# A chunk of V transposes moved ahead of the sum of exponents on TensorE

## The chip, the cores and the metric

The kernel runs on one core of one Trainium2 chip. The metric is device time in microseconds, the median of several executions of the same program. "Granted clock" is the share of TensorE's full speed that the throttle lets through.

## The reference

Attention for one query row and its backward pass: 32 heads, 8192 keys, head size 128, bf16.

```python
def _fwd_reference(q, k, v):
    scale = q.shape[-1] ** -0.5
    scores = jnp.einsum('bhqd,bhkd->bhqk', q, k) * scale
    attn = _softmax(scores, axis=-1)
    return jnp.einsum('bhqk,bhkd->bhqd', attn, v)
# outputs: out_0 = attention, out_1 = dq, out_2 = dk, out_3 = dv (for a given grad_out)
```

For each head K and V are read once (2 MB each), and dK and dV are written once (2 MB each). dK is an outer product of ds and q, dV an outer product of p and grad_out, so nearly all the bytes are these four tiles. PSUM is where the program has TensorE put its results; here ScalarE copies the transposed V out of it.

## The kernel before

One head is one turn of a loop, and the end of head h-1 (ds, dK, dq) is woven into the front of head h. The instruction order on each engine is the order of the program text. The parts that matter here:

```python
K_BUFS = 3
V_BUFS = 2
# ... PSUM pool for the transposed V: two buffers, psT ... bufs=2
def v_transposes(h, c):                        # c is one of four chunks of V
    T_ps = psT.tile([P, CH // 2, P], F32, tag="T", name="T_ps")
    # ... eight transposes on TensorE into T_ps
    X = tpool.tile([P, CH // 2, P], F32, tag="XT", name="XT_sb")
    nc.scalar.copy(X[:], T_ps[:])              # ScalarE empties the buffer
    XV[h, c] = X
# ... in the loop, for head h:
    nc.tensor.transpose(x["m"][:, 128:256], top[:].to_broadcast([P, P]), ident_f[:])  # row maxima
    # ... nbias (VectorE), then the exponent on ScalarE, with its row sums rs
    nc.scalar.activation(e[:], x["sn"], ACT.Exp, bias=nbias[:], scale=scale, accum_out=rs[:])
    nc.tensor.matmul(x["m"][:, 0:1], lhsT=ones_f[:], rhs=rs[:], ...)                  # sum of exponents
    # ... reciprocal rinv (VectorE), p = e * rinv (ScalarE), p_s (VectorE)
    v_transposes(h, 0)
    v_transposes(h, 1)
    v_transposes(h, 2)
    contract(Vt[h], x["p"], x["m"][:, 2:3])    # o = p V, 64 matmuls
    # ... v_scores (dp), v_transposes(h, 3), o . do, then dV products (VectorE) and the next V load
```

## Time and profile before

| what | before |
|---|---|
| time | 646.56 us, median of 3 (646.2 to 646.75) |
| TensorE, VectorE, ScalarE busy | 75%, 78%, 28% of the span |
| granted clock | 0.60 |
| bytes moved | 134.2 MB read, 134.2 MB written |
| transfers, most of the run | 422 to 433 GB/s |

No compute engine is busy all the time, the transfers are. Three rows of the view of the waits of the kernel before (who waited for whom: us in all, times, longest):

```profile
DVE G_dv L210 <- DMA out_dram<-G_dv: 84.6, 25, 4.6
...
PE s_ps L157 <- DVE pdt L234: 72.1, 24, 3.9
...
PE m_ps L294 <- ACT e L293: 40.5, 32, 1.3
```

The last row is the wait that the change aims at. The first two are larger and not touched by it.

### The profile page before, as it was taken

How to read it: one execution, taken by the hardware profiler on the slowest of the kernel's cores; microseconds unless marked ns; L12 is line 12 of the kernel's file. 1: busy time of each engine (PE TensorE's matmuls, PEld its weight loads, DVE VectorE, ACT ScalarE, POOL GpSimd, SP SyncE). 2: the span in 40 equal slices, each digit the busy share in tenths (PEclk: the TensorE clock that was granted, in tenths of full speed). 3: DMA queues.
4: the chain of work that ended last, by engine and by line, in shares of the span. 5: the costliest groups of instructions: out<-in, count | busy, mean ns of one | idle time of the engine just before them, and what ended most of it. 6: DMA issues, size and time to landing. Idle time of an engine off the chain costs nothing.

```text
span 644.5 us, 20935 instructions
## 1 busy us (share of the span) xinstructions
PE 481.0 (75%) x9673; PEld 452.0 (70%) x9673; DVE 505.5 (78%) x653; ACT 183.5 (28%) x332; POOL 0.7 (0%) x6
## 2 busy tenths in 40 slices
PE   3898888886677877768777787667786777877780
PEld 2888888886677866768666777667785676866670
DVE  5989899867977779777788777797767977778860
ACT  2333333332233222233222332223322223222230
POOL 0000000000000000000000000000000000000000
PEclk9766666655666655666556666556655666655665
DMA  8999999999999999999999999999999999999985
GB/s 349 407 425 430 424 425 423 429 426 431 427 428 427 427 427 429 429 429 425 433 422 433 425 430 427 427 429 425 427 429 425 431 425 429 429 427 430 424 365 238
DMA packets 19718, 269.80 MB, mean 419 GB/s; under 512 B 2352, under 2 KB 2352, under 8 KB 2864
## 3 DMA queue, kind: packets, MB, share of 16 engines
q1 hardware_dynamic: 19584, 268.47, 98.2%
q8 instruction: 75, 1.23, 0.7%
q14 instruction: 11, 0.09, 0.0%
q10 hardware_dynamic: 48, 0.01, 0.0%
HBM read 134.23 MB, written 134.23 MB: 417 GB/s over the span
## 4 chain that ended last, share of the span: by engine, by line
DMA 59%; PE 21%; DVE 14%; ACT 2%; issue 1%; SPq 0%; DVEq 0%; ACTq 0%
DMA Kt<-in_k_dram 48%; DVE XK_sb L146 8%; PE T_ps L183 8%; DMA out_dram<-G_dv 5%; DMA out_dram<-G_dk 5%; PE s_ps L157 5%; DVE G_dk L210 4%; PE dp_ps L200 3%; PE m_ps L200 2%; PE dp_ps L195 2%; ACT XT_sb L185 1%; PE m_ps L294 1%; DVE G_dv L210 1%; PE s_ps L173 1%; DVE sm L163 1%
## 5 line engine op out<-in xcount | busy, mean ns | idle before, releaser
L210 DVE TENSOR_TENSOR G_dv<-p_rep,qd 128x2048 bf16<-128x2048 bf16 x128 | 148.2, 1221 | 90.3 <-DMA out_dram<-G_dv 84.6
L183 PE MATMUL T_ps<-ident_f,Vt 128*128 128x128 f32 x1024 | 203.4, 382 | 0.2 <-PE m_ps L294 0.2
L183 PEld LDWEIGHTS T_ps<-ident_f,Vt 128*128 128x128 f32 x1024 | 190.7, 210 | 0.2 <-issue 0.2
L185 ACT COPY XT_sb<-T_ps 128x1024 f32<-128x1024 f32 x128 | 128.6, 1013 | 129.3 <-PE T_ps L183 127.2
L210 DVE TENSOR_TENSOR G_dk<-ds_rep,qd 128x2048 bf16<-128x2048 bf16 x128 | 155.6, 1218 | 2.9 <-DMA out_dram<-G_dk 1.9
L146 DVE STREAM_TRANSPOSE XK_sb<-Kt 128x1024 f32<-128x1024 f32 x128 | 148.3, 1214 | 5.8 <-DMA Kt<-in_k_dram 4.7
L157 PEld LDWEIGHTS <-XK_sb 128*128 128x128 bf16 x2048 | 57.7, 104 | 90.7 <-DVE pdt L234 79.9
L157 PE MATMUL s_ps<-q_blk,XK_sb 128*128 128x4 bf16 x2048 | 59.7, 168 | 82.1 <-DVE pdt L234 72.1
L195 PE MATMUL dp_ps<-do_blk,XT_sb 128*128 128x2 bf16 x2048 | 66.7, 164 | 18.1 <-ACT XT_sb L185 18.1
L195 PEld LDWEIGHTS <-XT_sb 128*128 128x128 bf16 x2048 | 64.9, 102 | 20.7 <-ACT XT_sb L185 20.7
L200 PE MATMUL dp_ps<-ds_rep,Kt 128*128 128x1 bf16 x2048 | 64.1, 165 | 1.3 <-issue 1.0
L200 PEld LDWEIGHTS <-Kt 128*128 128x128 bf16 x2048 | 59.6, 104 | 6.8 <-issue 6.6
L244 ACT COPY dq_all<-dp_ps 128x1 f32<-128x1 f32 x32 | 5.1, 159 | 192.4 <-PE dp_ps L200 178.5
L200 PEld LDWEIGHTS <-Vt 128*128 128x128 bf16 x2048 | 57.7, 97 | 0.9
L200 PE MATMUL m_ps<-p_rep,Vt 128*128 128x1 bf16 x2048 | 56.9, 164 | 0.0
L294 PEld LDWEIGHTS m_ps<-rs,ones_f 128*128 128x128 f32 x64 | 16.0, 311 | 49.9 <-ACT e L293 49.9
L294 PE MATMUL m_ps<-rs,ones_f 128*128 128x1 f32 x64 | 18.8, 362 | 40.5 <-ACT e L293 40.5
L303 ACT ACTIVATE p_rep<-e,rinv 128x256 bf16<-128x256 f32 x32 | 16.3, 508 | 30.1 <-DVE rinv L301 30.1
L163 DVE TENSOR_TENSOR sm<-s_ps,in_quad 128x256 f32<-128x256 f32 x32 | 13.6, 424 | 11.1 <-PE s_ps L157 7.9
L229 ACT CAST qd<-s_ps 128x256 bf16<-128x256 f32 x32 | 11.9, 372 | 32.2 <-PE s_ps L225 32.2
L236 DVE SCALAR_TENSOR_TENSOR ds_rep<-dp_ps,pdt,p_s 128x256 bf16<-128x256 f32 x32 | 15.5, 484 | 5.2 <-PE dp_ps L195 2.4
L293 ACT ACTIVATE e<-s_ps,nbias 128x64 f32<-128x64 f32 x32 | 10.0, 313 | 31.8 <-DVE nbias L290 31.8
(44 smaller groups left out, 143.4 us busy)
## 6 DMA issues: line engine op xcount, KB each, us to landing
Vt<-in_v_dram SPq DMA_DIRECT2D x32, 2048.0 KB, 30.0
Kt<-in_k_dram SPq DMA_DIRECT2D x31, 2048.0 KB, 30.8
out_dram<-G_dv SPq DMA_DIRECT2D x30, 2048.0 KB, 34.6
out_dram<-G_dk SPq DMA_DIRECT2D x30, 2048.0 KB, 33.6
out_dram<-G_dv SPq DMA_DIRECT2D x4, 1024.0 KB, 15.0
out_dram<-G_dk SPq DMA_DIRECT2D x4, 1024.0 KB, 13.3
Kt<-in_k_dram SPq DMA_DIRECT2D x4, 512.0 KB, 5.1
out_dram<-fin_sb SPq DMA_DIRECT2D x2, 8.0 KB, 13.1
```

What stands on the lines that cost most here:

```text
L146: nc.vector.transpose(XK[h][:, :, :, u, :], slots(Kt[h], u, NCH).rearrange("p g d -> p (g d)").bitcast(F32).rearrange("p (g w j) -> p g w ...
L157: nc.tensor.matmul(out[:, g, :], lhsT=cols[:, g, c // 2, c % 2], rhs=q_blk[:, h, c, :], start=(c == 0), stop=(c == 2 * NB - 1), skip_group ...
L163: nc.vector.tensor_tensor(x["sm"][:], x["s"][:, 0:NT].rearrange("p (a g) -> p a g", a=NQ).unsqueeze(2) .to_broadcast([P, NQ, NCH, CH]), in ...
L183: nc.tensor.transpose(T_ps[:, i, :], words[:, m * P:(m + 1) * P], ident_f[:])
L185: nc.scalar.copy(X[:], T_ps[:])
L195: nc.tensor.matmul(st[h]["dp"][:, n:n + 2], lhsT=X[:, i, e2, :], rhs=do_blk[:, h, e2, :], start=(e2 == 0), stop=(e2 == 1), skip_group_chec ...
L200: nc.tensor.matmul(out_col, lhsT=Xt[:, n, :], rhs=rep[:, n, 0:1], start=(n == 0), stop=(n == NT - 1), skip_group_check=True)
L210: nc.vector.tensor_tensor(slots(G, r, 4).rearrange("p n (a b) -> p n a b", b=R), slots(rep, r, 4).unsqueeze(2).to_broadcast([P, Q, D // R, ...
L229: nc.scalar.copy(x["qd"][:].rearrange("p a d -> p (a d)"), x["s"][:, 256:512])
L236: nc.vector.scalar_tensor_tensor(out=x["ds"][:], in0=x["dp"][:, 0:NT].unsqueeze(2).to_broadcast([P, NT, R]), scalar=pdt[:], in1=x["p_s"][: ...
L294: nc.tensor.matmul(x["m"][:, 0:1], lhsT=ones_f[:], rhs=rs[:], start=True, stop=True, skip_group_check=True)
L303: nc.scalar.activation(x["p"][:], e[:].unsqueeze(2).to_broadcast([P, NT, R]), ACT.Copy, scale=rinv[:])
```

## The change

TensorE stands still while ScalarE makes the exponent. The intent is to put eight V transposes into that gap, which need nothing of the softmax. Their copy out of PSUM must not stand in front of the p copy on ScalarE, so the copy is split off and stays where it was.

```diff
+    def v_copy(h, c):
+        X = tpool.tile([P, CH // 2, P], F32, tag="XT", name="XT_sb")
+        nc.scalar.copy(X[:], st[h].pop("T")[:])
+        XV[h, c] = X
-    def v_transposes(h, c):
+    def v_transposes(h, c, copy=True):
 ...
-        X = tpool.tile([P, CH // 2, P], F32, tag="XT", name="XT_sb")
-        nc.scalar.copy(X[:], T_ps[:])
-        XV[h, c] = X
+        st[h]["T"] = T_ps
+        if copy:
+            v_copy(h, c)
 ...
             nc.vector.tensor_reduce(nbias[:], x["m"][:, 128:256], axis=AX.X, op=ALU.max, negate=True)
+            v_transposes(h, 0, copy=False)
 ...
-        v_transposes(h, 0)
+        v_copy(h, 0)
         v_transposes(h, 1)
```

## The prediction

> **What bounds the kernel now.** I read the page from its chain and its slices first, then the DMA issues, then the cost groups of the lines that the change touches, then the timeline of one head and the busy time by stretches. The chain that ended last, the slices and the transfers:
>
> ```profile
> DMA  8999999999999999999999999999999999999985
> GB/s 349 407 425 430 424 425 423 429 426 431 427 428 427 427 427 429 429 429 425 433 422 433 425 430 427 427 429 425 427 429 425 431 425 429 429 427 430 424 365 238
> ...
> DMA 59%; PE 21%; DVE 14%; ACT 2%; issue 1%; SPq 0%; DVEq 0%; ACTq 0%
> ...
> Vt<-in_v_dram SPq DMA_DIRECT2D x32, 2048.0 KB, 30.0
> Kt<-in_k_dram SPq DMA_DIRECT2D x31, 2048.0 KB, 30.8
> out_dram<-G_dv SPq DMA_DIRECT2D x30, 2048.0 KB, 34.6
> ```
>
> The transfers run at 422 to 433 GB/s in slices 3 to 38 of 40, and a 2 MB load lands 30 us after it was issued. One head moves four such tiles (K, V, dK, dV): 4 x 2.097 MB / 428 GB/s = 19.6 us, and in the timeline the K transposes of consecutive heads begin 19.4 to 20.1 us apart (563.53, 582.97, 602.76). A tile alone needs 2.097 / 428 = 4.9 us, so 30 us are about six tiles in the queue: a backlog of 25 us that absorbs shifts of a microsecond in when a transfer is issued. The first six heads go at 17.25 us a head (K transposes at 21.04, 38.28, 55.53), held by compute, but they only eat the loads that were issued ahead; the slices show the transfers at full rate all the same.
>
> The groups that the change moves (line, engine, operation, count, busy us, mean ns, idle before):
>
> ```profile
> L183 PE MATMUL T_ps<-ident_f,Vt 128*128 128x128 f32 x1024 | 203.4, 382 | 0.2 <-PE m_ps L294 0.2
> L185 ACT COPY XT_sb<-T_ps 128x1024 f32<-128x1024 f32 x128 | 128.6, 1013 | 129.3 <-PE T_ps L183 127.2
> L294 PE MATMUL m_ps<-rs,ones_f 128*128 128x1 f32 x64 | 18.8, 362 | 40.5 <-ACT e L293 40.5
> ```
>
> TensorE waits 40.5 us over 32 heads, 1.27 us a head, for the exponent before the sum (L294). That is the gap that the change wants to fill. Head 30 in the timeline, a steady head:
>
> ```profile
> 563.52 0.34 SPq L78 DMA_DIRECT2D Vt<-in_v_dram  x1
> 591.56 0.48 PE L283 MATMUL m_ps<-ident_f,top 128*128 128x128 f32 x1
> 593.33 0.58 PE L294 MATMUL m_ps<-rs,ones_f 128*128 128x1 f32 x2 [1.29 <-ACT e L293]
> 593.77 5.36 PE L183 MATMUL T_ps<-ident_f,Vt 128*128 128x128 f32 x24
> 594.21 0.51 ACT L303 ACTIVATE p_rep<-e,rinv 128x256 bf16<-128x256 f32 x1 [0.94 <-DVE rinv L301]
> 597.95 4.63 DVE L210 TENSOR_TENSOR G_dv<-p_rep,qd 128x2048 bf16<-128x2048 bf16 x4 [3.47 <-DMA out_dram<-G_dv]
> 598.93 1.83 PE L200 MATMUL m_ps<-p_rep,Vt 128*128 128x1 bf16 x64
> ```
>
> The issue of this head's V stands in the first line. The view of that one transfer gives its time from issue to landing:
>
> ```profile
> DMA to landing us min/median/max: 29.3/29.3/29.3
> ```
>
> So V of head 30 landed at 563.52 + 29.3 = 592.8 us, but the transpose of the row maxima (L283) ended at 591.56 + 0.48 = 592.04. The moved chunk stands directly behind that transpose and needs V: **V is late by 0.8 us**. The same subtraction for every head gives V 0.6 to 1.4 us late in heads 7 to 31; only heads 0 to 6 have V early, by 0.3 to 10 us. The wait was invisible before, because the transposes stood behind the sum and started at 593.77.
>
> **What the Trainium skill says.** "DMA: Bandwidth & Descriptors", Specifications, gives a fabric ceiling of 435 GB/s for the 16 engines of a core; the trace's 428 GB/s is 98% of it, so there is no faster rate to be had by other timing. The same page, "Why a DMA increments its semaphore by 16 and not by 1", says that a transfer is done only when every engine that carries a part of it is done; the trace has no engine numbers, but the uneven end below fits. "TensorE: Matmul & The Clock Gate", Part 1, has a clock that is either half or full; the stretches show 0.50 and 1.00, and the chunk of eight transposes takes 1.07 us at 1.00 (at 621.95 us) and 1.7 us at 0.50 (614.31 us to the copy at 616.29, less 0.3 us of hand-over).
>
> **The change part by part.** The instruction order of the built kernel confirms: on TensorE eight transposes (chunk 0) move from behind the sum to between the maxima's transpose and the sum; ScalarE keeps its order (exponent, p copy, chunk 0 copy), since the copy of chunk 0 stood behind the p copy before too; VectorE's order is unchanged. Nothing is added or removed.
> - Steady head (times from the end of the maxima's transpose, before: sum at +1.29, first transposes +1.73, contraction at +6.9). After: chunk 0 waits for V to +0.8, runs 1.7 us to +2.5; the exponent was ready long before, so the sum is at +2.5, **1.2 us later**; chunk 1 from +2.95 to +4.65. Sum out at +3.1, reciprocal +3.4, p copy to +3.9, copy of chunk 0 (1.01 us) to +4.95. Chunk 2 needs the PSUM buffer that chunk 0 frees (two buffers), so it waits from +4.65 to +5.0 and ends at +6.6. Contraction at about +6.6: **0.3 us earlier**. p is 1.2 us later, but dV's VectorE work waits 3.47 us for the store of two heads ago anyway.
> - Early head (1 to 6): V is there, chunk 0 starts at once, sum 0.4 us later (1.7 - 1.29), contraction 0.3 to 0.4 us earlier. Here VectorE begins dV straight after p, so the dV products, the K transposes and ds come 0.4 us later, against only 0.2 us of VectorE idle before ds. The period may grow from 17.25 to about 17.5 us; five such heads, 1.5 us in all, go into the backlog, not into the time.
> - Last head: chunk 0 waits for V (1.1 us late), contraction 0 to 0.3 us earlier, and dK's products start at most that much earlier.
>
> The end, in stretches of the span (columns: PE, PEld, DVE, ACT, POOL busy, granted clock, DMA share, GB/s):
>
> ```profile
> 612.00:614.00 2.00, 0.64 (x3) 0.33 (x2) 2.00 (x4) 0.56 (x3) 0.00 (x0) 0.50 0.69 295
> 614.00:620.00 6.00, 6.00 (x45) 5.94 (x46) 2.25 (x5) 2.83 (x4) 0.00 (x0) 0.50 0.95 401
> 620.00:622.00 2.00, 2.00 (x84) 2.00 (x82) 2.00 (x2) 0.88 (x2) 0.00 (x0) 0.98 0.64 266
> ...
> 626.00:628.00 2.00, 1.48 (x46) 1.21 (x43) 2.00 (x3) 0.38 (x2) 0.00 (x0) 0.50 0.70 293
> 628.00:634.00 6.00, 0.00 (x0) 0.00 (x0) 1.96 (x2) 0.25 (x1) 0.00 (x0) 0.50 0.94 392
> 634.00:640.00 6.00, 0.00 (x0) 0.00 (x0) 0.00 (x0) 0.00 (x0) 0.00 (x0) 0.50 0.56 235
> ```
>
> Three times the queues run short (0.64 to 0.70), but never below about half, and from 634 to 640 us again about half of the engines work, 7 us after the other half is through. The likely reading: about nine engines are behind and never run dry, and they set the end. A dK issue that comes 0.3 us earlier then only feeds engines that finish early anyway. Sum: 0 us from the steady part, 0 to -0.3 us from the tail; 646.56 - 0.1 = 646.5 us.
>
> **The rivals.**
> 1. The gap is really gained: 1.27 us a head. For it: the 40.5 us of idle time. If it all counted, 606 us; but with transfers at 98% of their ceiling it can count only in the last head, whose chain from the landing of K (602.7) to the last product (630) is bare: at most 646.56 - 1.3 = 645.3 us. Against even that: V late, and the two PSUM buffers.
> 2. The wait for V starts a new chain: sum and p late by 1.2 us in 25 heads, then VectorE late, loads issued late. If nothing absorbed it, 646.6 + 25 x 1.2 = 677 us. Against it: 3.47 us of VectorE idle after p, a contraction that is not later, and 25 us of backlog.
> 3. The early heads slow down enough to starve the queue: 1.5 us at worst, 648 us. Against it: 430 GB/s in these slices.
>
> **Range and chances.** The runs before spread over 0.55 us (646.2 to 646.75). Rival 1 sets the low end, 645.3; rival 3 sets the high end, 647.8. Faster by 2% would need 633.6 us, which at 428 GB/s for 268.4 MB (627 us) leaves 6.5 us for start and tail, against some 19 now; slower by 2% needs 13 us that 25 us of backlog would have to let through. I give each 0.01.
>
> **What would show it.** In the changed trace: a new wait of TensorE for the V load before the first transposes, 0.6 to 1 us in some 25 heads, some 20 us in all; the idle time for the exponent before the sum near zero; a wait of 0.2 to 0.5 us a head before chunk 2 for ScalarE's copy; p later by about 1.2 us; VectorE's wait for the dV store shorter by about as much (84.6 us now, some 55 to 60 then); GB/s unchanged. Wrong would be: a contraction later than +7, slices below 420 GB/s in the steady part, or a tail in which all engines end together, earlier by over 0.5 us.

## The result, and the profile after

| what | before | after |
|---|---|---|
| time, median | 646.38 us of 4 (646.2 to 646.75) | 646.04 us of 4 (645.68 to 646.6) |
| ratio | | 0.9995, 95% interval 0.9977 to 1.0012 |
| span of the profiled run | 644.5 us | 644.6 us |

A ratio is the mean time of one kernel's runs over the mean of the other's runs of the same rounds, so it is not quite the ratio of the medians in the table. Executions over 1.5% slower than the fastest of the same kernel are left out of the means.

The page of the changed kernel (bytes per second by slice, chain, V transfers). Lines 188, 300 and 309 of the changed kernel are the transposes, the sum and the p copy, which were 183, 294 and 303:

```profile
GB/s 350 404 428 429 424 427 424 428 429 421 418 429 428 428 425 430 430 426 431 425 428 428 430 426 428 428 428 427 427 429 431 424 432 424 430 426 429 427 362 244
...
DMA 62%; PE 24%; DVE 9%; ACT 1%; issue 1%; SPq 0%; DVEq 0%; ACTq 0%
...
Vt<-in_v_dram SPq DMA_DIRECT2D x32, 2048.0 KB, 30.1
```

The rate by slice is about the same, and V still takes 30 us from issue to landing. Now the steady head 30 in the timeline of the changed kernel:

```profile
563.68 0.34 SPq L78 DMA_DIRECT2D Vt<-in_v_dram  x1
...
592.07 0.48 PE L288 MATMUL m_ps<-ident_f,top 128*128 128x128 f32 x1
...
593.32 1.94 PE L188 MATMUL T_ps<-ident_f,Vt 128*128 128x128 f32 x8 [0.77 <-DMA Vt<-in_v_dram]
...
595.05 0.42 PE L300 MATMUL m_ps<-rs,ones_f 128*128 128x1 f32 x2
...
598.17 4.63 DVE L215 TENSOR_TENSOR G_dv<-p_rep,qd 128x2048 bf16<-128x2048 bf16 x4 [2.13 <-DMA out_dram<-G_dv]
...
598.44 1.75 PE L205 MATMUL m_ps<-p_rep,Vt 128*128 128x1 bf16 x64
```

The eight transposes stand where they should, behind the transpose of the maxima, but wait 0.77 us for V. The sum comes 2.5 us after the maxima's transpose ends (592.55), where it was 1.29 us. VectorE's dV products then wait 2.13 us for the store of an earlier head where they waited 3.47. They begin when that store is done, whatever p does.

The view of the waits of the changed kernel, the rows that answer to the three above:

```profile
DVE G_dv L215 <- DMA out_dram<-G_dv: 52.8, 24, 3.6
...
PE s_ps L157 <- DVE pdt L239: 87.6, 31, 4.6
...
PE T_ps L188 <- DMA Vt<-in_v_dram: 24.7, 26, 2.5
```

The wait of the sum for the exponent is gone from the list. TensorE's two large waits were 72.1 + 40.5 = 112.6 us before and are 87.6 + 24.7 = 112.3 us now. **The idle time was not removed, it changed its name:** part of it is now a wait for V, and the rest a longer wait for VectorE before the K scores.

In the first six heads, where V is there early, the change does act. The timeline of the kernel before around the K scores of head 2 shows VectorE waiting twice in each head for TensorE (0.20 us at ds, in the prediction, and the row below):

```profile
45.85 0.42 DVE L163 TENSOR_TENSOR sm<-s_ps,in_quad 128x256 f32<-128x256 f32 x1 [0.97 <-PE s_ps L157]
```

In the changed kernel the same place of the loop has TensorE waiting for VectorE instead:

```profile
42.70 1.87 PE L157 MATMUL s_ps<-q_blk,XK_sb 128*128 128x4 bf16 x64 [1.03 <-DVE pdt L239]
```

The K transposes of heads 1, 2 and 3 begin at 21.64, 38.02 and 54.40 us, 16.38 us apart, where they were 17.25 us apart. Those heads are faster by 0.87 us. The lead does not last: head 3 takes 18.11 us, the lead is 1.3 us at head 5 (88.89 against 90.19 us), and at head 7 it is gone (125.59 and 125.62 us), where heads have come to be 19 us and more apart. The time is the same.

### The profile page after: what moved, and what is told of

It is laid out like the page before. It is cut to its first block, busy times and chain, and to the rows that moved or that the text cites. A ratio compares the mean times of both kernels' runs of the same rounds, so it can differ in the third digit from the quotient of the medians.

```text
span 644.6 us, 20935 instructions
## 1 busy us (share of the span) xinstructions
PE 482.0 (75%) x9673; PEld 443.9 (69%) x9673; DVE 505.9 (78%) x653; ACT 180.7 (28%) x332; POOL 0.7 (0%) x6
## 3 DMA queue, kind: packets, MB, share of 16 engines
q8 instruction: 75, 1.23, 0.7%
## 4 chain that ended last, share of the span: by engine, by line
DMA 62%; PE 24%; DVE 9%; ACT 1%; issue 1%; SPq 0%; DVEq 0%; ACTq 0%
DMA Vt<-in_v_dram 61%; PE T_ps L188 15%; DVE XK_sb L146 4%; DVE G_dv L215 4%; PE m_ps L205 3%; PE dp_ps L200 2%; PE s_ps L157 2%; PE dp_ps L205 1%; DVE G_dk L215 1%; DMA Kt<-in_k_dram 1%; PE m_ps L300 1%; ACT p_rep L309 0%; PE s_ps L173 0%; ACT XT_sb L179 0%; PE m_ps L288 0%
## 5 line engine op out<-in xcount | busy, mean ns | idle before, releaser
L188 PE MATMUL T_ps<-ident_f,Vt 128*128 128x128 f32 x1024 | 217.0, 383 | 27.3 <-DMA Vt<-in_v_dram 24.7
L188 PEld LDWEIGHTS T_ps<-ident_f,Vt 128*128 128x128 f32 x1024 | 182.2, 206 | 45.2 <-PE m_ps L288 21.7
L215 DVE TENSOR_TENSOR G_dv<-p_rep,qd 128x2048 bf16<-128x2048 bf16 x128 | 148.2, 1220 | 60.9 <-DMA out_dram<-G_dv 52.8
L157 PE MATMUL s_ps<-q_blk,XK_sb 128*128 128x4 bf16 x2048 | 59.8, 168 | 94.6 <-DVE pdt L239 87.6
L307 DVE RECIPROCAL rinv<-m_ps 128x1 f32<-128x1 f32 x32 | 5.4, 168 | 35.2 <-PE m_ps L300 35.1
L300 PEld LDWEIGHTS m_ps<-rs,ones_f 128*128 128x128 f32 x64 | 17.6, 334 | 0.0
## 6 DMA issues: line engine op xcount, KB each, us to landing
Vt<-in_v_dram SPq DMA_DIRECT2D x32, 2048.0 KB, 30.1
out_dram<-G_dk SPq DMA_DIRECT2D x4, 1024.0 KB, 13.2
```

Of the source, the lines that this page charges most:

```text
L157: nc.tensor.matmul(out[:, g, :], lhsT=cols[:, g, c // 2, c % 2], rhs=q_blk[:, h, c, :], start=(c == 0), stop=(c == 2 * NB - 1), skip_group ...
L188: nc.tensor.transpose(T_ps[:, i, :], words[:, m * P:(m + 1) * P], ident_f[:])
L215: nc.vector.tensor_tensor(slots(G, r, 4).rearrange("p n (a b) -> p n a b", b=R), slots(rep, r, 4).unsqueeze(2).to_broadcast([P, Q, D // R, ...
```

## The experiments

My theory after the result: the transfers set the time. They run at their ceiling from the third slice to the last 30 us, and even at the end the last stores wait behind others. TensorE's order is worth 0.87 us a head where transfers do not bind, and nothing where they do. Rivals: (1) the gain was real everywhere but was eaten by the late V or by the second PSUM buffer; (2) transfers are held back by compute and could go faster; (3) the bare chain of the last head sets the end.

### The transfers alone

Everything between the loads and the stores is left out, and there are five buffers for K and five for V. Its output is wrong, which doesn't matter for the time.

```diff
-    (all compute)
+    for h in range(H):
+        nc.sync.dma_start(rows_of(out_2, h, 0, 1), Kt[h][:])
+        nc.sync.dma_start(rows_of(out_3, h, 0, 1), Vt[h][:])
+        if h + 3 < H:
+            load_k(h + 3)
+            load_v(h + 3)
```

> The transfers alone: the same 2 MB loads of K and V and the same 2 MB stores of dK and dV, with no compute between (the result is wrong on purpose: K and V are stored as they were loaded). Theory (the transfers bind): 268.4 MB at 428 GB/s are 627 us, plus 2 us of start and 2 to 6 us at the end: 631 to 637 us, so that all compute in the kernel costs no more than its 10 to 15 us of tail. If the 7 us by which about nine engines lag at the end come from the loads of instructions, they are gone here, since this program has few instructions. Rival (the transfers are held back by compute's waits, and could run faster): clearly under 620 us.

Measured: 633.6 us (633.51 to 633.69), ratio 0.980 to the kernel before (0.9786 to 0.9815). The page, bytes per second by slice:

```profile
GB/s 335 431 423 431 428 431 432 430 429 429 429 432 431 426 432 431 429 432 429 431 432 432 432 432 432 432 432 432 432 432 432 431 432 432 432 431 432 432 431 303
```

As expected of the theory (whose own sum gives 631 to 635 us, not 637): rival 2 falls but for 2%, since with no compute at all the same bytes take 633.6 us. The changed kernel is 12.4 us above this floor, and an order of compute that leaves these transfers as they are can hardly win more than that. Two parts of the 12.4 us can be read. The end: the last two slices move 362 and 244 GB/s against 431 and 303 here, and 69 + 59 GB/s over slices of 16.1 us are 2.1 MB, or 4.8 us at 428 GB/s. The rate: some 427 against 431 GB/s. The page of the kernel before gives the instruction queue 75 packets and 0.7% of the 16 engines' span (0.7% of 644.5 is 4.5 us), and this program has none in that queue; that this is the reason of the lower rate fits in size but is not shown. That the lag between engines at the end would be gone here was only half right: the last packets still end over a stretch of some 4 us, against 9 us in the kernel before.

### A third V buffer

```diff
-V_BUFS = 2
+V_BUFS = 3
```

> The changed kernel with three V buffers instead of two, so that a V load may be issued one head earlier. Theory: V then lands before the moved chunk asks for it, TensorE's wait for the V load falls from 24.7 us to near 0, the sum comes 1.5 us after the maxima's transpose instead of 2.5 us, and the time still does not move: 645.5 to 647 us, ratio to the kernel before within 0.3%. Rival (the gain of the new order was eaten by the late V): the 0.8 us a head come back, 25 heads x 0.8 = 20 us, so some 626 us.

Measured: 645.90 us (645.64 to 647.95), ratio to the kernel before 1.0001 (0.9982 to 1.0020); correct. The time stays as the theory says, but **my expectation of the wait was wrong**. The wait for V, in the view of the waits:

```profile
PE T_ps L188 <- DMA Vt<-in_v_dram: 23.7, 26, 2.5
```

And the V transfers in the view of the issues:

```profile
Vt<-in_v_dram SPq DMA_DIRECT2D x32, 2048.0 KB, 38.3
```

V is issued some 8 us earlier, and takes 8 us longer (38.3 against 30.1 us), so it lands at the same point of the head: 0.6 us after the maxima's transpose in most heads, as in the changed kernel. The order of the transfers in the queue had not changed, and all bytes ahead of V still have to go at 428 GB/s. A buffer more makes the queue deeper, not faster. Since V was still late, this run does not test rival 1. The next two test its second half, the PSUM buffer. No run takes away the lateness of V alone; the transfers alone bound what it can have eaten, at 12.4 us.

### V never loaded, in both orders

The K tile stands in for V everywhere, so that a head moves three tiles instead of four. Their outputs are wrong, which doesn't matter for the times.

```diff
     Kt[h] = kpool.tile([P, NT, D], BF16, tag="K", name="Kt")
+    Vt[h] = Kt[h]
 ...
-    Vt[h] = vpool.tile([P, NT, D], BF16, tag="V", name="Vt")
-    nc.sync.dma_start(Vt[h][:], rows_of(v, h, 0, 1))
+    pass
```

> The kernel before with V never loaded: the tile of K stands for it everywhere (wrong result on purpose). Three tiles a head instead of four: transfers need 3 x 4.9 = 14.7 us a head, less than compute, so compute must bind. At the 17.25 us a head of the first six heads: last head starts at 21 + 30 x 17.25 = 538 us, and some 32 us follow: 565 to 575 us.

> The changed kernel with V never loaded, as in k_for_v_before. Theory after seeing the trace (early heads of the changed kernel go at 16.38 us, K transposes at 21.64, 38.02, 54.40): 22 + 30 x 16.38 + 32 = 545 us, 25 us or 4.4% faster than the same edit of the kernel before; the order is worth 0.87 us a head once transfers do not bind. Rival 1 (my prediction for early heads: the period grows to 17.5 us): 1.4% slower than k_for_v_before. Rival 2 (the second PSUM buffer's wait takes the gain away): equal within 1%.

Measured: 577.97 us (576.71 to 578.59) in the old order, 3 us above the range that I had expected, and 559.69 us (558.27 to 560.96) in the new. Their ratios to the kernel before are 0.8937 and 0.8657, so the new order is 0.8657 / 0.8937 = 0.969 of the old: 18.3 us or 3.1% faster. The waits in the old order, then in the new:

```profile
PE m_ps L294 <- ACT e L293: 38.8, 32, 1.3
...
DVE sm L163 <- PE s_ps L157: 30.3, 31, 2.0
```

```profile
PE s_ps L157 <- DVE pdt L239: 30.7, 30, 1.8
```

In the old order VectorE waits for TensorE in 31 heads, in the new one TensorE waits for VectorE in 30. The median distance of the K transposes of two heads is 17.24 us in the old order and 16.38 us in the new, 0.86 us apart, as in the early heads of the full kernels. So the change does what it was made for when transfers do not bind and V is not late (both are so here, and the two are not told apart), and the wait for the PSUM buffer does not take it away: rival 1's second half falls, and so does my own forecast of 17.5 us.

The size was smaller than expected (3.1% for 4.4%, 559.69 us for 545), because some heads of the new order take 17.8 to 19.2 us: the excess over the median adds up to 13.1 us there and to 3.4 us in the old order. In such heads TensorE stands still for up to 2.7 us, and the views put it down to "issue", which is to say that they name nothing that it waits for:

```profile
249.72 1.54 PE L188 MATMUL T_ps<-ident_f,Kt 128*128 128x128 f32 x6 [1.83 <-issue]
```

The DMA packets of the trace say more. A packet of the instruction queue q8 had ended at 248.47 us, 1.25 us before TensorE went on. So it is with all twelve such stalls of over 0.5 us, eight in the new order (13.2 us in all) and four in the old (5.5 us): each ends 1.2 to 1.6 us after a q8 packet, and these packets are some 7 us apart. The queue carries TensorE's program, as far as its count tells: 24 more transposes a head, with their weight loads 1536 instructions, raise it from 75 to 81 packets. The likely reading is that TensorE waits for its next instructions. The long head 3 of the changed kernel has the same mark: a stall that ends at 65.46 us, 1.47 us after such a packet. No run tests this, and why the packet is late in these heads alone stays open.

### More transposes in every head, in both orders

The last chunk of V is transposed four times over, which adds 24 transposes a head; the values are the same.

```diff
-        for i in range(CH // 2):
+        for i in [i for _ in range(4 if c == 3 else 1) for i in range(CH // 2)]:
```

> The kernel before with the eight transposes of the last chunk of V done four times over in every head (the same values are written, the result stays right): 24 more transposes, some 3.2 to 4.5 us of TensorE a head by its clock. This asks how much room the transfers leave. Before, TensorE's chain and VectorE's are within 0.2 us of each other at 17.25 us a head, so the period becomes 20.4 to 21.7 us against the transfers' 19.6: slower by 25 to 65 us (4 to 10%).

> The changed kernel with the same 24 more transposes in every head. Theory (the change did shorten TensorE's path, by 0.9 us a head or more, and the early heads then wait for VectorE with some 1.3 us of room on TensorE): period 16.4 + (3.2 to 4.5) - 1.3 = 18.3 to 19.6 us, at or under the transfers' 19.6: 646 to 652 us. Rival (the change bought no room, its chunk only waits elsewhere): as slow as the same edit of the kernel before, 670 us or more.

Measured: 680.59 us (678.72 to 690.95; the run of 690.95 us is slow and is left out of the ratio) in the old order, ratio 1.0526 (1.0501 to 1.0550); 655.53 us (654.36 to 656.77) in the new, ratio 1.0146 (1.0128 to 1.0164), which is clear of noise. Both results are correct. Most heads of the old order are 20.48 us apart, so the 24 transposes lengthen the period that compute sets by 20.48 - 17.24 = 3.24 us, and lift it over the transfers' 19.6 us. (My expectation had the two chains within 0.2 us of each other; VectorE's waits of 1.17 us a head, above, say otherwise.) The new order carries most of the same work under the transfers, 1.0146 / 1.0526 = 0.964 of the old. Its rival falls, but my figure was too good: 655.5 us lies above 646 to 652. The page of the new order, bytes per second by slice:

```profile
GB/s 350 405 421 401 396 422 415 408 425 425 427 428 426 427 430 427 426 427 425 425 427 427 427 430 427 427 430 424 426 429 426 424 428 429 426 426 421 395 347 174
```

Slices 3 to 8 move 396 to 422 GB/s, and heads 1 to 4 take 18.9 to 21.6 us. Of the 9.4 us by which its span is longer than the changed kernel's, 7.5 are there when head 16 begins (312.94 against 305.40 us); from there on its heads are 19.9 us apart on average, the changed kernel's 19.8. V is late in 6 heads only here (4.3 us in all), since TensorE comes to it later. **The change bought room, not time.**

### The last head alone made late

```diff
-        for i in range(CH // 2):
+        for i in [i for _ in range(4 if c == 3 and h == H - 1 else 1) for i in range(CH // 2)]:
```

> The changed kernel with the last chunk of V transposed four times over in the last head alone: dK's products and the last two stores come 3 to 5 us later, the result stays right. Theory (about nine engines are behind and set the end; they reach the last two stores only near 636 us, 6 us after these were issued): the time moves by 0 to 0.7 us. Rival (the bare chain of the last head sets the end): 3 to 5 us longer, 0.5 to 0.8%.

Measured: 645.86 us (645.44 to 646.43), ratio to the kernel before 0.9998 (0.9984 to 1.0013); correct. In the timeline the last dK products begin here:

```profile
628.70 4.63 DVE L215 TENSOR_TENSOR G_dk<-ds_rep,qd 128x2048 bf16<-128x2048 bf16 x4
```

The last K load landed at 601.97 us in this trace and at 602.89 in the changed kernel's, where these products begin at 625.74: they are 26.7 us behind K's landing instead of 22.9, so the delay is 3.9 us. The time does not move. From the issues and landings of the traces: the last store is issued at 633.36 us instead of 630.40, and lands at 642.52 instead of 643.38. In both traces this is 4.9 us after the landing of the last dV store (637.60 and 638.49), and 4.9 us is just what two megabytes need at 428 GB/s. The stretches show what takes up the slack (columns as in the prediction, the last two are DMA share and GB/s):

```profile
628.00:634.00 6.00, 2.44 (x72) 2.10 (x69) 5.11 (x5) 0.89 (x4) 0.00 (x0) 0.56 0.72 298
634.00:640.00 6.00, 0.00 (x0) 0.00 (x0) 0.00 (x0) 0.00 (x0) 0.00 (x0) 0.50 0.76 318
```

In the changed kernel these stretches have 0.93 (389 GB/s) and 0.58 (242 GB/s). Counted at single moments, 15 or 16 packets are in flight there to 633 us and 9 or 10 from 635 to 640; here 9 are from 628 to 631 and 16 or 17 from 632 to 636. The engines that were through early now work later, and the ones that were behind end when they ended. Rival 3 falls, for a delay of up to 3.9 us at least. Which engines are behind, and why, the trace does not say.

No run points to a version that beats both kernels: the time left above the floor is in the transfers of the end and in the rate, which this order does not touch.

## Why the prediction was right

The time (646.5 forecast, 646.04 measured) and the chances were right, and so was the reason: transfers at their ceiling. By its steps:

- **What bounds the kernel.** Confirmed by the transfers alone, 633.6 us, and by the two orders with V left out, which differ by 3.1% when the transfers have room. (Steady heads of the kernel before are up to 20.8 us apart, not 20.1.)
- **V late by 0.8 us.** Confirmed: 0.77 us in head 30, 24.7 us in 26 heads; "some 20 us in some 25 heads" was forecast. Reading when an operand lands, before moving its first use forward, found this.
- **Steady head.** Sum at +2.5 us and p later by 1.2 us were forecast; measured medians are +2.5 us, and p at +3.22 instead of +2.18, so 1.04 us later. VectorE's wait for the dV store was to fall from 84.6 us to 55 to 60, and fell to 52.8. The contraction was to come at +6.6, 0.3 us earlier than head 30's +6.9; in head 30 it came at +5.9. Chunk 2 waited 0.35 us for its PSUM buffer as forecast, but began 0.3 us sooner, and ran at a higher granted clock (1.13 us of weight loads for eight transposes, where I had counted 1.6 us at half clock). These two terms were mis-sized, in a part that does not set the time. One head is no measure here: over heads 7 to 31 the median is +6.7 before and +6.2 after. My sign of being wrong, a contraction later than +7, came in heads 14 and 24 (+7.2 and +7.3), where V was 2.2 and 2.3 us late; the time did not show it.
- **Early head: this step failed.** I wrote that "the period may grow from 17.25 to about 17.5 us"; it fell to 16.38 us. Two terms were wrong. p came 0.05 us later (+2.23 for +2.18), not 0.4: the first transposes start 0.2 us before the maxima's transpose ends, and the pipelined sum takes 0.42 us for 0.58. And I had counted "only 0.2 us of VectorE idle before ds" and had overlooked the 0.97 us that VectorE waits for the K scores two instructions later. With 0.97 + 0.20 = 1.17 us of waiting a head, VectorE was not the bound of the early heads; TensorE's chain was, and the change shortened that one by 0.87 us. The time did not feel it, because those heads only use up loads that were issued ahead.
- **Tail.** I forecast a contraction "0 to 0.3 us earlier", dK's products earlier by at most that, and no effect on the end. The contraction came 0.8 us earlier (+6.1 for +6.9), but dK's products 0.25 us later after the head's K transposes (22.82 for 22.57 us), since the last chunk of V took 1.84 us where it had taken 1.07: the granted clock was 0.54 over these transposes, and 1.00 in the kernel before. So the sign was wrong, and the end did not move. That the end does not hang on this chain is shown by the last head made late. The step from half-idle engines to "about nine engines set the end" fits the share of busy engines (0.58 in the last stretch) and the 9 or 10 packets in flight; that they are the same engines throughout, the trace does not say.
- **The rivals.** The gap gained in full: refuted in the full kernel, where the idle time moved, and true for 0.86 of the 1.27 us a head where transfers have room. The wait for V as a new chain: the wait was there, and the page's chain now even runs through the V loads (61% of the span), yet no cost of it shows in the time; in head 30 the store of an earlier head ends later. The starving early heads: they became faster.

## What to carry to other kernels

When the transfers run at their ceiling, a wait that is filled can come back under another name while the sum of the waits stays what it was (112.6 and 112.3 us here): look at what the whole program waits for before filling a gap. Before moving the first use of a loaded tile forward, subtract when it lands. And when a change is worth nothing, ask whether it bought room: here 3 us more work a head cost 5.3% in the old order and 1.5% in the new.

## What the Trainium skill lacked or had wrong

- "Runtime: NRT & Kernel Launch", Instruction fetch mechanics, calls the cost of crossing a 16 KiB block of instructions "mostly hidden". In a program bound by transfers the blocks use the same engines: the page counts 75 packets and 1.23 MB in the instruction queue, and they take 0.7% of all 16 engines' span, some 4.5 us an engine. The program without them ran at 431 to 432 GB/s, the kernel at some 427; that the one causes the other was not tested alone. With V left out, TensorE stood still for 0.6 to 2.7 us eight times in the new order and 1.1 to 1.7 us four times in the old, each time until 1.2 to 1.6 us after such a block had ended; that it waited for the block was not tested either.
- "TensorE: Matmul & The Clock Gate", Part 4, says that the full clock does not engage for transposes. In the run with the late last head nothing but 32 transposes of 32-bit words (MATMUL in the trace) ran on TensorE from 621.07 to 626.27 us, and the granted clock was 0.94 from 621 to 622 us, 0.50 from 622 to 625, 0.85 from 625 to 626 and 1.00 from 626 to 627. With 24 more transposes a head the mean granted clock rose from 0.60 to 0.755.
- "DMA: Bandwidth & Descriptors", Bandwidth, has load rates only. Loads and stores mixed half and half, 2 MB each, ran at 423 to 432 GB/s in slices 2 to 39 of the transfers alone.
- No page spells out that a load issued earlier into a full queue lands no earlier: with a third V buffer the issue moved by 8 us and the time to landing from 30.1 to 38.3 us.
